# Three engines' instructions issued in the order in which the program writes them: agent attention with a cosine feed-forward on Trainium2

## The chip, the cores and the metric

The kernel runs on one core of a Trainium2 chip. The time is device microseconds of one execution. Before the change it was 1285.07 us (median of 3 runs, 1277.71 to 1285.25).

The core's engines have names in the profile: PE is TensorE (matmuls), PEld its weight loads, DVE is VectorE, ACT is ScalarE, POOL is GpSimd, SP is SyncE, which here issues the DMAs. Each engine takes its own instructions one after the other; an instruction whose input is not ready holds up all that stand behind it on that engine. Engines wait for each other through semaphores.

## What is computed

Cut to what matters, with B = 4 batches, N = 12480 tokens, 128 channels, 49 agents and 2048 hidden units:

```python
def sm(a, b):                       # a softmax of scaled scores
    s = scale * (a @ b.transpose(0, 2, 1))
    s = s - s.max(-1, keepdims=True)
    e = np.exp(s)
    return e / (e.sum(-1, keepdims=True) + 1e-09)

agent_v = sm(agents, k) @ v         # (B, 49, 128)
x = (sm(q, agents) @ agent_v).reshape(B * N, 128)
h = x @ w_in                        # (49920, 2048)
out = (h * np.cos(h)) @ w_out
```

## The kernel before

**Tiles and steps.** Tokens are taken in groups of 960 (`GRP`; 13 groups a batch, 52 in all), each in two chunks of 480 columns. The product of `agent_v` and `w_in` is formed once a batch (`a`), so that a chunk of `h` is one matmul from the 49 softmax weights (`pT`) to 128 hidden units. A step handles 256 hidden units of one chunk: 8 steps a chunk, 16 a group, 208 a batch, 832 in all, and 4 more (`LAG`) to run out. Step n does this (lines 549 to 586):

- TensorE: two matmuls into a `ph` tile (line 558). There are three `ph` tiles in PSUM, so step n needs the one that step n-3 has left.
- ScalarE: the sine with a shift of pi/2, `cos` (line 561), from `ph`.
- VectorE: `r` = (cos - 1) * h (line 563), from `cos` and `ph`. It is the last reader of `ph`.
- `plan.run(n)`: what the plan put at this step (below).
- TensorE: two matmuls of `r` of step n-4 with `w_out` into `po` (line 579). `po` gathers 8 steps; the first of them has none and the second has four, the last adds two correction matmuls (lines 576, 577), then ScalarE copies `po` to `osb` (line 581) and SP stores it.

**The plan.** Everything else of later groups and of the next batch is cut into pieces and put at steps by a schedule written out by hand (lines 465 to 546; `plan`, `extra`, `spread_out`, `burst`). Here a "piece of scores" or "of values" means:

- keys (`ab[b].scores`, line 167): 8 score matmuls a group (16 PE instructions, line 102), half of them in one step and half in the next; ScalarE copies them to `s` (line 181), VectorE keeps a running maximum (line 192);
- queries (`query`, line 351): the same matmuls, then VectorE's maximum and subtraction (lines 360, 367);
- values (`ab[b].values`, line 234): 16 PE instructions (line 244), then VectorE adds the result to `av` (line 247 or 249);
- turned weights (`query_turned`, line 386): four transposes, a ScalarE copy, GpSimd's copies into `pT`, seven steps before the group begins.

All of these results go through the `one` tiles, of which PSUM has two (line 320). `po` holds one of them for most of a chunk, so the pieces share the other, one after the other.

**Bursts.** The exponentials need another ScalarE table than the sine, so they are bundled: at steps 108, 132 and 156 of each of the first three batches (`BURSTS`) stand one exponential of a third of the keys (`pinned_exp`) and one of four or five groups of queries (`query_exp`), with a table load before and after. VectorE's sums over the queries' exponentials (`query_sums`, lines 375 to 377) are planned one step later. Behind the second and the third burst stand four whole pieces of values at four steps on end (line 522), behind the third five more in halves. Two smaller bursts, of queries alone, stand at steps 19 and 732.

**Who sets the order.** The order of the source is not the order on an engine. A scheduler (Tile's) takes the traced instructions and issues each when its modelled inputs and tile buffers are ready, with earlier ones preferred; the semaphores follow from the order that it settles on. `tc.keep_in_program_order(ins)` puts an instruction behind the one that was traced before it on the same engine: an edge for the order of issue, no wait for its end. Before the change it is used for the exponentials (lines 371, 399, 404), and for the loads up to step 7 (line 80).

Of the kernel before, what the change touches and what calls it, by code (L numbers as in the profile page):

```python
# [18 lines left out]
P = 128  # L19
# [21 lines left out]
def agent_attention_cos_ffn(ctx, tc, qT, kT, v, agT, w_in, w_out, outT):  # L41
# [32 lines left out]

    pinned = [True]
# [18 lines left out]
    def scores(sb, src, b, ps):  # L94

        xt = sb.tile([P, GRP], F32, name="xt", bufs=3)
        load(xt, src)
        ps = ps[:TT, :GT * NA].rearrange("p (t a) -> p t a", a=NA)
        for t in range(GT):
            if t == HT:  # L100
                yield
            nc.tensor.matmul(ps[:, t, :], xt[:, t * TT:(t + 1) * TT], ag[:, b, :], start=True, stop=True)  # L102
        return ps

    def scores_twice(xt, src, b, ps):

        load(xt, src)
        ps = ps[:TT, :, :HT * 2 * NA].rearrange("p h (t x a) -> p h t x a", x=2, a=NA)
        for t in range(GT):
            nc.tensor.matmul(ps[:, t // HT, t % HT], xt[:, t * TT:(t + 1) * TT], twice(ag[:, b, :]),  # L110
                             start=True, stop=True)
        return ps[:, :, :, 0, :]

    class Weights:
# [6 lines left out]
        def single(self, src, out):  # L121
# [5 lines left out]
            nc.vector.tensor_scalar(ex, hi, 20, 0x7FF, op0=ALU.logical_shift_right, op1=ALU.bitwise_and)  # L127
            nc.vector.tensor_scalar(man, hi, 0xFFFFF, 0x100000, op0=ALU.bitwise_and, op1=ALU.bitwise_or)
            nc.vector.tensor_scalar(ex, ex, 1151.0, 896.0, op0=ALU.min, op1=ALU.max)
            f = man.bitcast(F32)  # L130
            nc.vector.scalar_tensor_tensor(f, lo, 2.0 ** -32, man, op0=ALU.mult, op1=ALU.add)
            nc.vector.tensor_scalar(ex, ex, 896.0, 2.0 ** 23, op0=ALU.subtract, op1=ALU.mult)
            nc.vector.scalar_tensor_tensor(f, f, 2.0 ** -20, ex.bitcast(F32), op0=ALU.mult, op1=ALU.mult)
            nc.vector.scalar_tensor_tensor(out.bitcast(U32), hi, 0x80000000, man, op0=ALU.bitwise_and, op1=ALU.bitwise_or)
# [5 lines left out]
        def w_out(self, c):  # L140
# [3 lines left out]
            nc.scalar.copy(w1[:, fs], w)  # L144
            return w

        def product(self, c, w, po, wio):

            pt = self.psum()
            for t in range(4):  # L150
                f = slice((4 * c + t) * P, (4 * c + t + 1) * P)
                nc.tensor.transpose(pt[:, t * P:(t + 1) * P], win[:, f], ident)
            wt = self.sb.tile([P, 4, P], F32, name="wt", bufs=2)
            nc.scalar.copy(wt.rearrange("p f d -> p (f d)"), pt)
            for t in range(4):
                nc.tensor.matmul(po, wt[:, t], w[:, t], start=(c == t == 0), stop=(4 * c + t == NF - 1))
            if 4 * c + 4 == NF:
                nc.vector.tensor_copy(wio, po)

    class Agents:  # L160
# [6 lines left out]
        def scores(self, g):  # L167
# [11 lines left out]
            if self.wide is None:  # L179
                ps = yield from scores(sb, src, self.b, self.psum())  # L180
                nc.scalar.copy(s, ps)
            else:
# [5 lines left out]
                nc.scalar.copy(s.rearrange("p (h t) a -> p h t a", h=2), ps)  # L188
            if g == 0:
                nc.vector.tensor_copy(self.run, s)  # L190
            else:
                nc.vector.tensor_max(self.run, self.run, s)  # L192
# [7 lines left out]
        def top(self):  # L200
            self.m = self.sb.tile([TT, NA], F32, name="m", bufs=1)
            nc.vector.tensor_reduce(self.m, self.run.rearrange("p t a -> p a t"), axis=AX.X, op=ALU.max)

        def across(self):
            pt = self.psum()
            nc.tensor.transpose(pt[:NA, :TT], self.m, ident[:TT, :TT])
            mx = self.sb.tile([NA, 1], F32, name="mx", bufs=1)
            nc.vector.reduce_max(mx, pt[:NA, :TT], axis=AX.X)
            self.mxw = self.sb.tile([NA, TT], F32, name="mxw", bufs=1)
            nc.vector.tensor_copy(self.mxw, mx.to_broadcast([NA, TT]))  # L210

        def spread(self):
            pb = self.psum()
            nc.tensor.matmul(pb[:TT, :NA], self.mxw, ident[:NA, :NA], start=True, stop=True)
            self.mxb = self.sb.tile([TT, NA], F32, name="mxb", bufs=1)
            nc.vector.tensor_copy(self.mxb, pb[:TT, :NA])  # L216
# [5 lines left out]
        def exp(self, g, n):  # L222
            e = self.part(g, n)
            return nc.scalar.activation(e, e, AF.Exp, scale=SC)  # L224

        def add(self, g):

            on = nc.vector if self.wide else nc.gpsimd
# [5 lines left out]
        def values(self, g):  # L234
# [6 lines left out]
            for t in range(GT):  # L241
                if t == HT:
                    yield
                nc.tensor.matmul(po, vt[:, t, :], twice(e[:, t, :]), start=(t == 0 and (g == 0 or not lone)),  # L244
                                 stop=(t == GT - 1 and (g == NG - 1 or not lone)))
            if g == (NG - 1 if lone else 0):
                nc.vector.tensor_copy(self.sums, po)
            elif not lone:
                nc.vector.tensor_add(self.sums, self.sums, po)  # L249

        def total(self):
# [3 lines left out]
            nc.vector.tensor_reduce(self.es2[:, :NA], self.es.rearrange("p t a -> p a t"), axis=AX.X, op=ALU.add)  # L255
            nc.vector.tensor_copy(self.es2[:, HI:], self.es2[:, :NA])

        def inverse(self):

            pa = self.psum()  # L260
            nc.tensor.matmul(pa[:KR, :1], self.es2, ones[:TT], start=True, stop=True)
            z = self.sb.tile([KR, 1], F32, name="z", bufs=1)
            nc.vector.tensor_scalar_add(z, pa[:KR, :1], EPS)
            self.rz = self.sb.tile([KR, 1], F32, name="rz", bufs=1)
            nc.vector.reciprocal(self.rz, z)
# [3 lines left out]
    class Fast(Agents):  # L269

        def project(self, c, a):
# [3 lines left out]
            nc.tensor.matmul(pw[:KR], self.av, win[:, cs], start=True, stop=True)  # L275
            if c == 0:
                self.big = self.sb.tile([KR, DFF // 512], F32, name="big", bufs=1)
            nc.scalar.activation(a[:, cs], pw[:KR], AF.Copy, scale=self.rz)
            x = a[:, cs].bitcast(F32)
            nc.vector.tensor_reduce(self.big[:, c:c + 1], x, axis=AX.X, op=ALU.max, apply_absolute_value=True)  # L280

            on = nc.vector if self.wide else nc.gpsimd
            on.tensor_scalar(a[:, cs], x, FAST_MAX, -FAST_MAX, op0=ALU.min, op1=ALU.max)

        def project_out(self, wio, b1, b2):

            pw = self.psum()
            nc.tensor.matmul(pw[:KR, :P], self.av, wio, start=True, stop=True)
            nc.scalar.activation(b1, pw[:KR, :P], AF.Copy, scale=self.rz)
            nc.vector.scalar_tensor_tensor(b2, pw[:KR, :P], self.rz, b1.bitcast(F32), op0=ALU.mult, op1=ALU.subtract)  # L290

        def judge(self):

            t = self.sb.tile([KR, 1], F32, name="t", bufs=1)
            nc.vector.reduce_max(t, self.big, axis=AX.X)
            nc.vector.tensor_scalar(fits[:, self.b:self.b + 1], t, FAST_MAX, None, op0=ALU.is_le)
# [20 lines left out]
    with ExitStack() as pools:  # L317
# [33 lines left out]
        def query(n, piece, wide=False):  # L351
# [8 lines left out]
            nc.vector.reduce_max(mx, ps, axis=AX.X)  # L360
# [6 lines left out]
            nc.vector.tensor_sub(e_of[n].rearrange("p (h t) a -> p h t a", h=2), ps,  # L367
# [5 lines left out]
        def query_sums(piece):  # L373
            rz = rz_of[piece]
            nc.vector.reduce_sum(rz, e_of[piece], axis=AX.X)
            nc.vector.tensor_scalar_add(rz, rz, EPS)
            nc.vector.reciprocal(rz, rz)
# [8 lines left out]
        def query_turned(n):  # L386

            pt = small()
            for t in range(HT):
                nc.tensor.transpose(pt[:KR, t * TT:(t + 1) * TT], p_in[n % 2][:, t, :KR], ident[:TT, :TT])  # L390
            p = sb.tile([KR, CH], F32, name="p")
            nc.scalar.copy(p, pt[:KR, :CH])  # L392
# [8 lines left out]
        def sine_table():  # L401

            t = sb.tile([1, 1], F32, name="sine", bufs=1)
            tc.keep_in_program_order(nc.scalar.activation(t, half_pi[:1], AF.Sin))
# [23 lines left out]
        for j, (g, n) in enumerate(lots):  # L428
            for k in range(g, g + n):
                pre(NG + 2 + k, ab[0].shift, k, 1, nc.vector)  # L430
# [119 lines left out]
        for n in range(NSTEP + LAG):  # L550
            pinned[0] = n < NP
            if n < NSTEP:
# [3 lines left out]
                for j in range(2):  # L556
                    f = slice((2 * i + j) * P, (2 * i + j + 1) * P)
                    nc.tensor.matmul(ph[:, j, :CH], ai[:, f], pTs[q % 3][:, c], start=True, stop=True)  # L558
                h = ph[:, :, :CH]
                cos = sb.tile([P, 2, CH], F32, name="c", bufs=3)  # L560
                nc.scalar.activation(cos, h, AF.Sin, bias=half_pi, scale=1.0)  # L561
                r = rs[n] = sb.tile([P, 2, CH], F32R, name="r", bufs=6)
                nc.vector.scalar_tensor_tensor(r, cos, 1.0, h, op0=ALU.subtract, op1=ALU.mult)  # L563
# [10 lines left out]
            if i == NP - 1:  # L574
                k = q // NG % 2
                nc.tensor.matmul(po, b1[k], pTs[q % 3][:, c], start=False, stop=False)  # L576
                nc.tensor.matmul(po, b2[k], pTs[q % 3][:, c], start=False, stop=False)  # L577
            for f in range(0 if i == 1 else 2 * i, 2 * i + 2):
                nc.tensor.matmul(po, w1[:, f, :], rs[m - i + f // 2][:, f % 2, :], start=(f == 0), stop=(f == NF - 1))  # L579
            if i == NP - 1:  # L580
                nc.scalar.copy(osb[:, c * CH:(c + 1) * CH], po)  # L581
# [6 lines left out]

        bx = sb.tile([KR, 1], F32, name="bx", bufs=1)
        nc.vector.tensor_reduce(bx, fits, axis=AX.X, op=ALU.min)  # L590
        pt = small()
        nc.tensor.transpose(pt[:1, :KR], bx, ident[:KR, :KR])
# [134 lines left out]
```

## Time and profile before

| | |
|---|---|
| median of the runs | 1285.07 us |
| the profiled execution, its own time | 1283.99 us |
| its span, first to last instruction | 1282.0 us |
| before the first matmul of step 0 | 78.3 us |
| granted TensorE clock, mean | 0.966 of full speed |
| PE busy | 1193.2 us (93%) |
| DVE busy | 1096.7 us (86%) |
| ACT busy | 1030.2 us (80%) |
| POOL busy | 316.7 us (25%) |

How to read the lines that are quoted below. A page line of a group is: line of the kernel, engine, operation, tile written and tiles read, shapes, count, then busy time, mean nanoseconds of one, idle time just before them and what ended it. A line of the chain of waits is: who waited for whom, total us, times, the longest. A line of the timeline is: start, duration, engine, line, operation, count when several are merged, and in brackets the idle time before and what ended it. A line of windows is: stretch, its length, then busy time of PE, PEld, DVE, ACT and POOL with counts, the granted clock, the DMA share, GB/s. A matmul of float32 scores shows as two instructions.

### The profile page before, as it was taken

Reading aid. Unit: us, or ns where it says so; the run is one execution under the profiler, and the core shown is the slowest. Engines: PE = TensorE matmul, PEld = TensorE weight load, DVE = VectorE, ACT = ScalarE, POOL = GpSimd, SP = SyncE. Lnnn points to the kernel's source line nnn. Section 1 sums busy time; section 2 is a strip of 40 time slices with the busy share of each in tenths; the row PEclk is TensorE's granted clock in tenths of the full one; section 3 lists DMA queues with packets and bytes.
Section 4 is the critical chain, followed back from the end, with each engine's and each line's share of the span. In section 5 each row is a group of like instructions: output and inputs, shape, how many; then the busy total and the mean of one; then the engine's idle time right before and its main releaser. Section 6 shows DMA issues by size and latency. Waiting matters only on the chain.

```text
span 1282.0 us, 17196 instructions
## 1 busy us (share of the span) xinstructions
PE 1193.2 (93%) x6349; PEld 976.8 (76%) x6349; DVE 1096.7 (86%) x1217; ACT 1030.2 (80%) x1130; POOL 316.7 (25%) x341
## 2 busy tenths in 40 slices
PE   8898999989999999988999999998999999998997
PEld 8787878778887777777888777777778777676664
DVE  6877887788788988879888988887888999998997
ACT  2447887878788877876988888876897999999997
POOL 1202121332222212142422213116241321212220
PEclk9988998989899999998999999997999999998999
DMA  8962323124431223322242222232322010000000
GB/s 306 244 172 76 92 94 93 62 65 126 119 92 62 77 77 94 93 77 77 78 117 74 72 87 80 71 118 62 107 64 63 31 48 31 16 31 16 31 31 34
DMA packets 31016, 107.72 MB, mean 84 GB/s; under 512 B 3436, under 2 KB 3820, under 8 KB 30924
## 3 DMA queue, kind: packets, MB, share of 16 engines
q1 hardware_dynamic: 30924, 106.54, 27.0%
q8 instruction: 52, 0.85, 0.3%
q14 instruction: 40, 0.33, 0.1%
HBM read 80.97 MB, written 25.56 MB: 83 GB/s over the span
## 4 chain that ended last, share of the span: by engine, by line
PE 64%; ACT 14%; DVE 13%; issue 7%; DMA 1%; ACTq 0%; SPq 0%; DVEq 0%
PE ph L558 22%; PE one L579 18%; PE one L102 12%; DVE r L563 10%; ACT c L561 10%; PE one L244 4%; ACT osb L581 2%; PE ph L244 2%; PE one L576 2%; PE one L577 2%; PE ph L110 1%; PE one L390 1%; DVE mx L360 1%; DMA vt<-v 1%; ACT p L392 1%
## 5 line engine op out<-in xcount | busy, mean ns | idle before, releaser
L563 DVE SCALAR_TENSOR_TENSOR r<-c,ph 128x960 fp32r<-128x960 f32 x832 | 929.4, 1149 | 110.1 <-ACT c L561 107.0
L561 ACT ACTIVATE c<-ph,half_pi 128x960 f32<-128x960 f32 x832 | 864.9, 1067 | 172.2 <-PE ph L558 162.0
L558 PE MATMUL ph<-pT,a 113*128 113x480 f32 x1664 | 550.8, 412 | 31.9 <-DVE r L563 28.6
L579 PE MATMUL one<-r,w 128*128 128x480 f32 x1664 | 515.0, 395 | 13.1 <-ACT osb L581 12.0
L558 PEld LDWEIGHTS ph<-pT,a 113*128 113x128 f32 x1664 | 287.3, 194 | 129.8 <-DVE r L563 54.2
L579 PEld LDWEIGHTS one<-r,w 128*128 128x128 f32 x1664 | 317.9, 194 | 71.7 <-ACT osb L581 22.6
L102 PEld LDWEIGHTS one<-ag,xt 128*120 128x120 f32 x1408 | 178.2, 192 | 40.3 <-ACT osb L581 15.1
L102 PE MATMUL one<-ag,xt 128*120 128x49 f32 x1408 | 178.0, 271 | 13.8 <-ACT osb L581 7.6
L381 POOL TENSOR_TENSOR p<-e,rz 120x392 f32<-120x392 f32 x52 | 44.8, 867 | 532.4 <-PE one L390 426.4
L396 POOL TENSOR_TENSOR pT<-p,pT 49x480 fp32r<-49x480 f32 x104 | 127.1, 1222 | 7.9
L395 POOL CAST pT<-p 49x480 fp32r<-49x480 f32 x104 | 63.5, 611 | 167.9 <-ACT p L392 164.4
L244 PEld LDWEIGHTS one<-s,vt 120*128 120x128 f32 x624 | 79.7, 191 | 13.9 <-DVE av L249 6.9
L244 PE MATMUL one<-s,vt 120*128 120x98 f32 x624 | 81.1, 272 | 6.6 <-DVE av L249 4.5
L581 ACT COPY osb<-one 128x480 f32<-128x480 f32 x104 | 57.5, 553 | 4.5 <-PE one L579 4.4
L232 POOL TENSOR_TENSOR es<-es,s 120x392 f32<-120x392 f32 x36 | 36.7, 1019 | 71.5 <-ACT s L224 69.1
L220 POOL TENSOR_TENSOR s<-s,mxb 120x1568 f32<-120x1568 f32 (+1 forms) x9 | 31.6, 3537 | 63.6 <-DVE mxb L216 63.6
L390 PEld LDWEIGHTS one<-ident,p 120*113 120x113 f32 x208 | 31.3, 178 | 17.3 <-ACT osb L581 9.4
L360 DVE TENSOR_REDUCE mx<-one 120x8 f32<-120x392 f32 x49 | 27.5, 562 | 17.6 <-PE one L102 17.2
L390 PE MATMUL one<-ident,p 120*113 120x120 f32 x208 | 36.6, 275 | 6.0 <-ACT osb L581 4.1
L576 PE MATMUL one<-pT,b 113*128 113x480 f32 x104 | 41.3, 397 | 0.0
L577 PE MATMUL one<-pT,b 113*128 113x480 f32 x104 | 40.8, 392 | 0.0
L192 DVE TENSOR_TENSOR run<-run,s 120x392 f32<-120x392 f32 x48 | 27.7, 577 | 5.5 <-ACT s L188 3.1
(91 smaller groups left out, 513.3 us busy)
## 6 DMA issues: line engine op xcount, KB each, us to landing
xt<-qT SPq DMA_DIRECT2D x52, 480.0 KB, 3.5
vt<-v SPq DMA_DIRECT2D x52, 480.0 KB, 4.3
outT<-osb SPq DMA_DIRECT2D x51, 480.0 KB, 2.6
xt<-kT SPq DMA_DIRECT2D x46, 480.0 KB, 3.5
c<-kT SPq DMA_DIRECT2D x6, 480.0 KB, 5.2
raw<-w_in SPq DMA_DIRECT2D x4, 512.0 KB, 5.1
raw<-w_out SPq DMA_DIRECT2D x4, 512.0 KB, 9.1
outT<-osb SPq DMA_DIRECT2D x2, 240.0 KB, 2.7
```

The costliest lines, as they stand in the source:

```text
L102: nc.tensor.matmul(ps[:, t, :], xt[:, t * TT:(t + 1) * TT], ag[:, b, :], start=True, stop=True)
L244: nc.tensor.matmul(po, vt[:, t, :], twice(e[:, t, :]), start=(t == 0 and (g == 0 or not lone)), stop=(t == GT - 1 and (g == NG - 1 or not ...
L390: nc.tensor.transpose(pt[:KR, t * TT:(t + 1) * TT], p_in[n % 2][:, t, :KR], ident[:TT, :TT])
L395: nc.gpsimd.tensor_copy(pT[own, c], p[own])
L396: nc.gpsimd.tensor_sub(pT[other, c], p[own], pT[own, c].bitcast(F32))
L558: nc.tensor.matmul(ph[:, j, :CH], ai[:, f], pTs[q % 3][:, c], start=True, stop=True)
L561: nc.scalar.activation(cos, h, AF.Sin, bias=half_pi, scale=1.0)
L563: nc.vector.scalar_tensor_tensor(r, cos, 1.0, h, op0=ALU.subtract, op1=ALU.mult)
L576: nc.tensor.matmul(po, b1[k], pTs[q % 3][:, c], start=False, stop=False)
L577: nc.tensor.matmul(po, b2[k], pTs[q % 3][:, c], start=False, stop=False)
L579: nc.tensor.matmul(po, w1[:, f, :], rs[m - i + f // 2][:, f % 2, :], start=(f == 0), stop=(f == NF - 1))
L581: nc.scalar.copy(osb[:, c * CH:(c + 1) * CH], po)
```

## The change

From step 0 of the loop on, every instruction that the kernel gives to TensorE, VectorE or ScalarE is put behind the one that was traced before it on its engine. A thin wrapper does it; all calls on the three engines in the functions concerned go through it. What is computed, the tiles, the plan and its steps are the same. GpSimd's instructions and the DMAs (from step 8 on) stay with the scheduler, and so does all that comes ahead of step 0 and behind the loop.

```diff
+    class InOrder:
+        def __init__(self, engine):
+            self.engine = engine
+
+        def __getattr__(self, name):
+            f = getattr(self.engine, name)
+
+            def g(*args, **kwargs):
+                ins = f(*args, **kwargs)
+                if in_order[0]:
+                    tc.keep_in_program_order(ins)
+                return ins
+
+            return g
+
+    in_order = [False]
+    tensor = InOrder(nc.tensor)
+    vector, scalar = InOrder(nc.vector), InOrder(nc.scalar)
...
-                nc.tensor.matmul(po, vt[:, t, :], twice(e[:, t, :]), start=(t == 0 and (g == 0 or not lone)),
+                tensor.matmul(po, vt[:, t, :], twice(e[:, t, :]), start=(t == 0 and (g == 0 or not lone)),
...
             rz = rz_of[piece]
-            nc.vector.reduce_sum(rz, e_of[piece], axis=AX.X)
-            nc.vector.tensor_scalar_add(rz, rz, EPS)
-            nc.vector.reciprocal(rz, rz)
+            vector.reduce_sum(rz, e_of[piece], axis=AX.X)
+            vector.tensor_scalar_add(rz, rz, EPS)
+            vector.reciprocal(rz, rz)
...
         for n in range(NSTEP + LAG):
             pinned[0] = n < NP
+            in_order[0] = True
             if n < NSTEP:
...
-                    nc.tensor.matmul(ph[:, j, :CH], ai[:, f], pTs[q % 3][:, c], start=True, stop=True)
+                    tensor.matmul(ph[:, j, :CH], ai[:, f], pTs[q % 3][:, c], start=True, stop=True)
...
-                nc.scalar.activation(cos, h, AF.Sin, bias=half_pi, scale=1.0)
+                scalar.activation(cos, h, AF.Sin, bias=half_pi, scale=1.0)
...
-                nc.vector.scalar_tensor_tensor(r, cos, 1.0, h, op0=ALU.subtract, op1=ALU.mult)
+                vector.scalar_tensor_tensor(r, cos, 1.0, h, op0=ALU.subtract, op1=ALU.mult)
...
         assert not plan.at
 
+        in_order[0] = False
```

More of the change, by code (lines that the diff above doesn't have):

```diff
@@ L101, in scores @@
                 yield
-            nc.tensor.matmul(ps[:, t, :], xt[:, t * TT:(t + 1) * TT], ag[:, b, :], start=True, stop=True)
+            tensor.matmul(ps[:, t, :], xt[:, t * TT:(t + 1) * TT], ag[:, b, :], start=True, stop=True)
         return ps
@@ L109, in scores_twice @@
         for t in range(GT):
-            nc.tensor.matmul(ps[:, t // HT, t % HT], xt[:, t * TT:(t + 1) * TT], twice(ag[:, b, :]),
+            tensor.matmul(ps[:, t // HT, t % HT], xt[:, t * TT:(t + 1) * TT], twice(ag[:, b, :]),
                              start=True, stop=True)
@@ L187, in scores @@
                 ps = scores_twice(xt, src, self.b, self.wide())
-                nc.scalar.copy(s.rearrange("p (h t) a -> p h t a", h=2), ps)
+                scalar.copy(s.rearrange("p (h t) a -> p h t a", h=2), ps)
             if g == 0:
-                nc.vector.tensor_copy(self.run, s)
+                vector.tensor_copy(self.run, s)
             else:
-                nc.vector.tensor_max(self.run, self.run, s)
+                vector.tensor_max(self.run, self.run, s)
         def copies(self, x):
@@ L403, in sine_table @@
             t = sb.tile([1, 1], F32, name="sine", bufs=1)
-            tc.keep_in_program_order(nc.scalar.activation(t, half_pi[:1], AF.Sin))
+            tc.keep_in_program_order(scalar.activation(t, half_pi[:1], AF.Sin))
         ab = [Fast(sb, small, b, None if b else pair) for b in range(NB)]
@@ L575, in agent_attention_cos_ffn @@
                 k = q // NG % 2
-                nc.tensor.matmul(po, b1[k], pTs[q % 3][:, c], start=False, stop=False)
-                nc.tensor.matmul(po, b2[k], pTs[q % 3][:, c], start=False, stop=False)
+                tensor.matmul(po, b1[k], pTs[q % 3][:, c], start=False, stop=False)
+                tensor.matmul(po, b2[k], pTs[q % 3][:, c], start=False, stop=False)
             for f in range(0 if i == 1 else 2 * i, 2 * i + 2):
-                nc.tensor.matmul(po, w1[:, f, :], rs[m - i + f // 2][:, f % 2, :], start=(f == 0), stop=(f == NF - 1))
+                tensor.matmul(po, w1[:, f, :], rs[m - i + f // 2][:, f % 2, :], start=(f == 0), stop=(f == NF - 1))
             if i == NP - 1:
-                nc.scalar.copy(osb[:, c * CH:(c + 1) * CH], po)
+                scalar.copy(osb[:, c * CH:(c + 1) * CH], po)
                 at = q * GRP
```

92 lines of the change are left out of this document (46 added, 46 removed).

## The prediction

> **What bounds the kernel now.** I read the page's busy times first, then the table of waits, then windows and timelines of three kinds of stretches.
>
> ```profile
> PE 1193.2 (93%) x6349; PEld 976.8 (76%) x6349; DVE 1096.7 (86%) x1217; ACT 1030.2 (80%) x1130; POOL 316.7 (25%) x341
> ```
>
> ```profile
> ACT c L561 <- PE ph L558: 162.0, 267, 4.2
> DVE r L563 <- ACT c L561: 107.0, 236, 1.8
> PE ph L558 <- DVE r L563: 28.6, 59, 4.5
> ```
>
> Three engines are nearly full and wait for each other in a ring: ACT for PE's `ph`, DVE for ACT's `cos`, PE for DVE's `r`. No single engine is the bound; the ring is. Its size comes from a timeline.
>
> ```profile
> 608.54 0.68 PE L558 MATMUL ph<-pT,a 113*128 113x480 f32 x2
> 609.26 1.06 ACT L561 ACTIVATE c<-ph,half_pi 128x960 f32<-128x960 f32 x1 [1.39 <-PE ph L558]
> 610.36 1.16 DVE L563 SCALAR_TENSOR_TENSOR r<-c,ph 128x960 fp32r<-128x960 f32 x1 [1.30 <-ACT c L561]
> ...
> 1208.32 6.57 DVE L563 SCALAR_TENSOR_TENSOR r<-c,ph 128x960 fp32r<-128x960 f32 x6 [0.18 <-ACT c L561]
> ...
> 1212.01 0.59 PE L558 MATMUL ph<-pT,a 113*128 113x480 f32 x2
> 1212.44 0.59 PE L579 MATMUL one<-r,w 128*128 128x480 f32 x2
> ```
>
> From the start of `ph` to the start of its `r` is 610.36 - 608.54 = 1.82 us. With r's own 1.16 and some 0.1 of handing over (an estimate), `ph` of step n, which needs r of step n-3, gives r of step n some 3.1 us after r of n-3 began. Six r in 6.57 us are 1.06 to 1.1 apart, three of them 3.2 to 3.3. So PE may be late with a `ph` by 0.1 to 0.2 us; more shows in the time. A pair of these matmuls takes 0.43 to 0.44 us of PE (1212.01 to 1212.44).
>
> ```profile
> 454.50:548.80 94.30, 89.53 (x506) 74.41 (x506) 80.04 (x84) 75.79 (x86) 17.66 (x19) 1.00 0.31 95
> 1202.30:1265.80 63.50, 60.50 (x251) 42.88 (x251) 61.10 (x57) 60.80 (x67) 11.59 (x13) 1.00 0.08 32
> ```
>
> The second stretch holds steps 768 to 823 without pieces: 63.5 / 56 = 1.134 us a step. The first holds steps 240 to 303 with 14 pieces of scores: 94.3 - 64 x 1.134 = 21.7 us, so a piece costs 1.55 us now.
>
> The third kind is a burst, here the second of a batch (step 340), from the r of step 340 at 610.36:
>
> ```profile
> 610.35 1.28 ACT L224 ACT_TABLE_LOAD   x1
> 611.64 1.51 ACT L224 ACTIVATE s<-s 120x1568 f32<-120x1568 f32 x1
> 612.36 1.92 PE L244 MATMUL one<-s,vt 120*128 120x98 f32 x16
> 613.06 1.50 ACT L371 ACTIVATE e<-e 120x1568 f32<-120x1568 f32 x1
> 614.58 1.28 ACT L561 ACT_TABLE_LOAD   x1
> 614.59 1.79 DVE L375 TENSOR_REDUCE rz<-e 120x32 f32<-120x1568 f32 x1
> 614.63 2.03 PE L244 MATMUL one<-s,vt 120*128 120x98 f32 x16
> 615.87 2.97 ACT L561 ACTIVATE c<-ph,half_pi 128x960 f32<-128x960 f32 x3
> 616.69 0.26 DVE L249 TENSOR_TENSOR av<-av,one 128x98 f32<-128x98 f32 x1 [0.32 <-PE one L244]
> 616.87 0.17 DVE L376 TENSOR_SCALAR rz<-rz 120x32 f32<-120x32 f32 x1
> 617.01 2.03 PE L244 MATMUL one<-s,vt 120*128 120x98 f32 x16 [0.35 <-DVE av L249]
> 617.08 0.35 DVE L377 RECIPROCAL rz<-rz 120x32 f32<-120x32 f32 x1
> 617.35 4.43 DVE L563 SCALAR_TENSOR_TENSOR r<-c,ph 128x960 fp32r<-128x960 f32 x4
> ...
> 621.86 1.15 DVE L563 SCALAR_TENSOR_TENSOR r<-c,ph 128x960 fp32r<-128x960 f32 x1
> ```
>
> ACT makes no cosine for 1.28 + 1.51 + 1.50 + 1.28 = 5.57 us. What matters is what the others do meanwhile. PE runs the values of steps 342, 343 and 344 (the three rows of line 244), which the program writes behind `ph` of those steps. DVE does the sums (lines 375 to 377), which the program writes behind the r of step 341, at 617.35. The scheduler has moved work into the shadow of the burst: from r of 340 to r of 345 pass only 11.5 us.
>
> **The change part by part.** It adds no instruction and no semaphore of its own; it takes the scheduler's freedom on three engines. The four parts:
>
> *Second bursts (steps 132, 340, 548).* In program order DVE has r of 341 ahead of the sums and of the `av` addition, and PE has values 342 ahead of the `po` of step 338 and `ph` of 343. Values 342 need the `one` tile that values 341 used (the other holds `po`), so the `av` addition of 341; that stands behind the sums, those behind r of 341, that behind the cosine after the burst. Behind it on PE waits `ph` of 343, and ACT and DVE for that. In the trace's own times: cosine 341 at 615.87, r 341 at 617.0, sums from 618.1 for 1.79 + 0.17 + 0.35 = 2.3 to 620.4, `av` to 620.6. Values 342 take 1.85 (612.36: 16 in 1.92 with the last one's tail) to 622.5, `po` 0.44, `ph` 343 at 622.95, its r at +1.82 = 624.8. Values 343 run 623.4 to 625.2, `ph` 344 starts 625.65, r 344 at 627.5; values 344 wait for the addition behind r 343 (624.8 + 1.06 + 0.26 = 626.1), end 627.9, `ph` 345 starts 628.35, r 345 at 630.2. It is at 621.86 now: +8.3 us.
>
> *Third bursts (156, 364, 572).* The same with four pieces of values at 365 to 368.
>
> ```profile
> 649.08 2.20 DVE L375 TENSOR_REDUCE rz<-e 120x40 f32<-120x1960 f32 x1 [0.91 <-ACT e L371]
> 650.36 2.97 ACT L561 ACTIVATE c<-ph,half_pi 128x960 f32<-128x960 f32 x3
> ...
> 656.46 2.20 DVE L563 SCALAR_TENSOR_TENSOR r<-c,ph 128x960 fp32r<-128x960 f32 x2
> ```
>
> Cosine 365 at 650.36 gives r at 651.5, the sums run 652.5 to 655.2, `av` to 655.5, and from there to the r of the fourth step after it, 9.6 us as above (620.6 to 630.2): r of 369 at 665.1 instead of 656.46, +8.6 us. Both kinds in three batches: 3 x 16.9 = +51 us. Bounds: +26, if only the sums and one piece of values leave the shadow (2.3 to 2.7 and 1.85, some 4.4 a burst); +56, if each of some eight hand-overs behind a burst takes 0.1 more than I allow.
>
> *Other bursts.* Behind the three first ones stand queries, not values: the sums (2.3) come after r instead of in the shadow, and two pieces that PE now runs early stay at their steps. But the order of now loses there too, with PE waiting for a load (below: 1.31, issue). I take +2 each, +6, between -3 and +5 each. At steps 19 and 732 the sums leave the shadow, 2.3 to 2.9: +6, between 0 and +8.
>
> *All other pieces (103: 39 keys, 49 queries, 15 halved values).* A step with half a piece takes PE 0.44 + 0.86 + 0.44 = 1.74 us, where r's pace is 1.06. Set `ph` of n at 0, just as r of n-3 ends. `ph` of n+1 starts at 1.74, its r at 3.56 instead of 3.09; `ph` of n+2 at 3.48, its r at 5.3 instead of 4.15: late by 1.15. With a query's maximum and subtraction in between, 1.5. A piece that begins three steps after a query waits about 1.0 more for the `one` tile; that is about every eighth. Mean 1.45, against 1.55 now: 103 x -0.1 = -10. Bounds: 0.9 a piece (PE is ahead by more than I allow) is -67, 1.75 is +20. Steps without pieces keep their pace, set by r and the ring in either order: 0. The cover there is DVE's own 1.06; without it a step would have PE's 0.88.
>
> *The clock.* A long wait of PE costs twice.
>
> ```profile
> 573.93 2.93 PE L102 MATMUL one<-ag,xt 128*120 128x49 f32 x16 [1.31 <-issue]
> ...
> 1162.74 2.14 PE L558 MATMUL ph<-pT,a 113*128 113x480 f32 x4 [4.45 <-DVE r L563]
> ```
>
> After 4.45 us of waiting four matmuls take 2.14 us, where two pairs at full clock take 0.44 + 0.6; sixteen score matmuls take 2.93, not 1.85. In the second and third bursts PE now has values to run and the clock stays whole, as the granted clock, 1.00, of the stretch shows:
>
> ```profile
> 610.36:621.86 11.50, 11.15 (x74) 9.88 (x73) 8.44 (x12) 10.60 (x10) 4.09 (x4) 1.00 0.60 163
> ```
>
> In program order PE stands from about 613 (values 341, `po`, `ph` 342 done) to 620.6. So values 342 and the two pairs behind them come at half clock: 1.1 + 0.9 = +2.0 us, six times, +12; between 0 and +20.
>
> On this the Trainium skill, "TensorE: Matmul & The Clock Gate", section "Why this matters for your kernels", says to leave no gaps of over some 3 us between matmuls, since an idle window brings the half clock back. The trace agrees at 1162.74. The page's Part 1 on the clock gate gives the way back as one busy window of about 3.4 us; by that a stretch would lose half of 3.4, an estimate from the page of +1.7 instead of my +2.0, and the sum would be 1347. The same skill, "PSUM — Partial Sum Buffer", section "Engine vs sequencer instructions", says that matmuls start and complete in program order and that the other engines' queues are strict first in, first out; it speaks against the change, as nothing in the chip makes up for an order that has a waiting instruction ahead.
>
> Sum: 51 + 6 + 6 - 10 + 12 = +65 us on the profiled execution's 1284.0 (span 1282.0 and 2.0 around it): 1349 us, 5% slower. The median of the runs is 1.1 above that execution, which changes nothing at this size.
>
> **The rivals.**
>
> *Faster, by an even order.* The plan puts a piece in halves so that no `ph` is over 0.9 us late. The scheduler runs 16 at once:
>
> ```profile
> 550.99 1.88 PE L102 MATMUL one<-ag,xt 128*120 128x49 f32 x16 [0.30 <-ACT osb L581]
> 553.41 3.05 ACT L561 ACTIVATE c<-ph,half_pi 128x960 f32<-128x960 f32 x3 [1.50 <-PE ph L558]
> ```
>
> ACT then waits 1.50, and 162.0 us in all. If halves fit into the ring's slack, a piece costs VectorE's own work, 0.8 us: 103 x -0.75 = -77, and PE, then ahead, has less to catch up behind bursts: half of 51. 1284 + 26 + 12 - 77 = 1245. It decides the sign from about 1.5 us of slack in the ring. Against it: 3.1 against 3.2 to 3.3 us leaves 0.2.
>
> *No change.* The pieces gain what the bursts lose (0.9 a piece), or the edges bind where the scheduler had that order anyway: 1285. Against it: the values and sums named above stand in another order now.
>
> *Worse.* The half clock lasts through the values (16 in 2.93: four pieces +4 a burst, not 2), first bursts cost +5, pieces 1.75: 1284 + 56 + 15 + 8 + 20 + 24 = 1407.
>
> **How the numbers follow.** The forecast, 1310 to 1390 with the inner bounds of its terms: 0.72. Worse, 1390 and up: 0.11. No change: 0.06. Faster: 0.11. The range 1300 to 1390 leaves out about 0.2. Slower by over 1% (about what a measurement of this kernel tells from no change): 0.72 + 0.11 = 0.83; within 1%: 0.06; faster: 0.11.
>
> **What would show it.** In the changed profile, from r of step 340 to r of step 345: about 20 us instead of 11.5, with the sums behind the first r after the burst, and only one piece of values ahead of that r. A line in the waits in which PE at line 244 waits for `av` with several us at a time, and more of ACT's wait for `ph`. A granted clock below 1 in the stretch behind step 340, where it is 1.00 now. Steps 768 to 823 at 1.13 us as before. I am wrong if r of 340 to r of 345 stays under 14 us, or if steps 240 to 303 take under 85 or over 100 us.

## The result, and the profile after

| | before | after |
|---|---|---|
| median of the runs | 1285.16 us (4 runs) | 1366.42 us (4 runs, 1359.72 to 1369.91) |
| ratio | | 1.0637 [1.0575, 1.0699] |
| profiled execution, its span | 1282.0 us | 1362.2 us |
| granted TensorE clock, mean | 0.966 | 0.936 |
| time at half clock, 2 x (1 - clock) x span | 87 us | 174 us |

Slower, by 80.2 us of span. The prediction was 1349 us, +65, within 1300 to 1390. Ratios here and below are those on record, with their 95% interval; they are taken from undisturbed runs alone and can differ a little from the ratio of two medians.

One thing first on how to read what follows: every instruction that goes through the wrapper has the wrapper's line, L85, in the profile. The tiles tell them apart: `ph<-pT,a` is a step's first matmul pair, `one<-r,w` the pair into `po`, `one<-s,vt` the values, `one<-ag,xt` the scores, `rz` the sums, `av` the addition of the values.

The page's busy line, then the table of waits of the kernel after:

```profile
PE 1211.8 (89%) x6349; PEld 997.8 (73%) x6349; DVE 1095.0 (80%) x1217; ACT 1024.2 (75%) x1130; POOL 314.3 (23%) x341
```

```profile
ACT c L85 <- PE ph L85: 242.7, 243, 8.6
DVE r L85 <- ACT c L85: 204.5, 191, 6.1
...
PE one L85 <- DVE av L85: 48.7, 6, 8.7
...
PE one L85 <- DVE m L85: 11.2, 4, 3.3
...
PEld one L85 <- DVE es L85: 10.1, 3, 3.4
```

The engines did the same work in a longer span. The line that stands out is `PE one <- DVE av`: 48.7 us in six waits, 8.1 each, one for each second and third burst (before, 4.5 us in six waits). ACT's wait for `ph` grew from 162.0 to 242.7 and DVE's for the cosine from 107.0 to 204.5: the ring hands the wait on.

Where the time went is read best from one whole batch, between the same steps of both kernels. Windows of the kernel before (r of step 304 to 316, 316 to 336, 386 to 392, and the whole batch 208 to 416; the others stand in the prediction), then of the kernel after (240 to 304, 304 to 316, 316 to 336, 340 to 345, 364 to 369, 386 to 392, 208 to 416, and the quiet 768 to 824):

```profile
548.79:567.95 19.16, 17.01 (x85) 13.30 (x84) 16.37 (x22) 13.41 (x16) 5.86 (x2) 0.91 0.16 53
567.95:603.83 35.88, 31.86 (x156) 26.17 (x156) 28.53 (x33) 26.96 (x27) 17.81 (x17) 0.86 0.23 69
...
679.94:687.98 8.04, 8.04 (x39) 6.62 (x39) 7.39 (x11) 7.19 (x9) 0.96 (x3) 1.00 0.37 122
...
413.48:720.88 307.40, 290.23 (x1576) 240.26 (x1576) 263.87 (x286) 255.33 (x278) 84.28 (x86) 0.98 0.28 84
```

```profile
482.71:572.31 89.60, 86.78 (x507) 74.71 (x505) 80.16 (x85) 74.14 (x86) 16.97 (x19) 1.00 0.32 98
572.31:593.94 21.63, 17.83 (x80) 14.52 (x80) 15.76 (x19) 13.11 (x16) 7.46 (x3) 0.84 0.15 52
593.94:635.25 41.31, 35.04 (x170) 29.02 (x170) 29.31 (x34) 28.09 (x28) 16.19 (x16) 0.83 0.23 69
...
639.69:662.38 22.69, 15.17 (x87) 13.82 (x86) 8.70 (x12) 10.69 (x10) 4.59 (x5) 0.77 0.32 94
...
683.83:707.21 23.38, 14.69 (x86) 13.52 (x86) 9.07 (x12) 11.35 (x10) 5.54 (x6) 0.78 0.27 73
...
731.94:744.43 12.49, 9.53 (x38) 7.25 (x38) 8.74 (x12) 7.33 (x9) 0.20 (x1) 0.86 0.26 79
...
442.01:776.03 334.02, 298.62 (x1578) 248.92 (x1577) 263.43 (x285) 253.34 (x278) 83.44 (x86) 0.93 0.25 77
...
1284.49:1346.20 61.71, 60.33 (x252) 43.11 (x250) 60.51 (x57) 61.23 (x67) 11.67 (x13) 1.00 0.08 33
```

| steps of the batch | before | after | difference |
|---|---|---|---|
| 240 to 304, keys | 94.25 | 89.60 | -4.65 |
| 304 to 316, the maximum's round trip | 19.16 | 21.63 | +2.5 |
| 316 to 336, first burst and what follows | 35.88 | 41.31 | +5.4 |
| 340 to 345, second burst | 11.50 | 22.69 | +11.2 |
| 364 to 369, third burst | 12.26 | 23.38 | +11.1 |
| 386 to 392, the total's round trip | 8.04 | 12.49 | +4.45 |
| the other five stretches | 126.3 | 122.9 | -3.4 |
| 208 to 416 | 307.40 | 334.02 | +26.6 |

The three batches with bursts lost 26.0, 26.6 and 28.0 us, the time ahead of the first r grew by 2.5, and the last batch gained 3.0: together +80.1, with the span at +80.2. (The batches differ in detail: the second burst of the third one takes 22.68 instead of 11.95, its third burst 23.38 instead of 12.24; steps 732 to 737 take 13.7 instead of 10.1.)

The second burst in the timeline of the kernel after, from just before the r of step 340 (639.69). It answers to the burst shown in the prediction:

```profile
639.12 1.92 PE L85 MATMUL one<-s,vt 120*128 120x98 f32 x16
639.67 1.28 ACT L85 ACT_TABLE_LOAD   x1
...
645.19 2.01 ACT L85 ACTIVATE c<-ph,half_pi 128x960 f32<-128x960 f32 x2
646.28 1.16 DVE L85 SCALAR_TENSOR_TENSOR r<-c,ph 128x960 fp32r<-128x960 f32 x1 [5.44 <-ACT c L85]
647.36 1.78 DVE L85 TENSOR_REDUCE rz<-e 120x32 f32<-120x1568 f32 x1
...
649.65 0.20 DVE L85 COPY av<-one 128x98 f32<-128x98 f32 x1
649.77 1.14 DVE L85 SCALAR_TENSOR_TENSOR r<-c,ph 128x960 fp32r<-128x960 f32 x1
649.91 3.73 PE L85 MATMUL one<-s,vt 120*128 120x98 f32 x16 [7.52 <-DVE av L85]
655.09 2.59 PE L85 MATMUL one<-s,vt 120*128 120x98 f32 x16
655.33 1.06 ACT L85 ACTIVATE c<-ph,half_pi 128x960 f32<-128x960 f32 x1 [8.13 <-PE ph L85]
...
658.42 1.92 PE L85 MATMUL one<-s,vt 120*128 120x98 f32 x16
...
662.38 1.15 DVE L85 SCALAR_TENSOR_TENSOR r<-c,ph 128x960 fp32r<-128x960 f32 x1 [1.35 <-ACT c L85]
```

Only one piece of values (639.12) runs while ScalarE makes no cosine. The sums (647.36) and the copy to `av` (649.65) stand behind the first r after the burst. PE waits 7.52 us for that copy, since the next values need its `one` tile; `ph` of step 343 stands behind those values, and so ACT waits 8.13 for it. The values then take 3.73 and 2.59 us, where the last piece takes 1.92.

### The profile page after: what moved, and what is told of

The parts are those of the page before. It is cut to its first block, busy times and chain, and to the rows that moved or that the text cites. A ratio compares the mean times of both kernels' runs of the same rounds, so it can differ in the third digit from the quotient of the medians.

```text
span 1362.2 us, 17172 instructions
## 1 busy us (share of the span) xinstructions
PE 1211.8 (89%) x6349; PEld 997.8 (73%) x6349; DVE 1095.0 (80%) x1217; ACT 1024.2 (75%) x1130; POOL 314.3 (23%) x341
## 4 chain that ended last, share of the span: by engine, by line
PE 58%; DVE 21%; ACT 14%; issue 5%; DMA 1%; ACTq 0%; SPq 0%; DVEq 0%
PE one L85 36%; PE ph L85 22%; DVE r L85 15%; ACT c L85 9%; DVE rz L85 2%; ACT L85 2%; ACT osb L85 1%; DVE e L85 1%; ACT e L391 1%; DVE mx L85 1%; ACT p L85 1%; DMA vt<-v 1%; DVE es L85 0%; DMA raw<-w_out 0%; DVE big L85 0%
## 5 line engine op out<-in xcount | busy, mean ns | idle before, releaser
L85 DVE SCALAR_TENSOR_TENSOR r<-c,ph 128x960 fp32r<-128x960 f32 x832 | 920.1, 1150 | 216.1 <-ACT c L85 204.5
L85 ACT ACTIVATE c<-ph,half_pi 128x960 f32<-128x960 f32 x832 | 859.8, 1068 | 247.5 <-PE ph L85 242.7
L85 PE MATMUL ph<-pT,a 113*128 113x480 f32 x1664 | 541.4, 409 | 50.0 <-DVE r L85 42.4
L85 PE MATMUL one<-r,w 128*128 128x480 f32 x1664 | 520.9, 405 | 1.4 <-ACT osb L85 1.3
L85 PEld LDWEIGHTS ph<-pT,a 113*128 113x128 f32 x1664 | 302.7, 197 | 170.3 <-DVE r L85 87.7
L85 PEld LDWEIGHTS one<-r,w 128*128 128x128 f32 x1664 | 308.4, 196 | 47.0 <-issue 5.0
L85 PEld LDWEIGHTS one<-ag,xt 128*120 128x120 f32 x1408 | 180.1, 190 | 31.2 <-PE ph L85 13.8
L85 PE MATMUL one<-ag,xt 128*120 128x49 f32 x1408 | 173.4, 267 | 11.9 <-PE ph L85 9.7
L85 PE MATMUL one<-s,vt 120*128 120x98 f32 x624 | 91.3, 302 | 48.7 <-DVE av L85 48.7
L85 PEld LDWEIGHTS one<-s,vt 120*128 120x128 f32 x624 | 89.9, 220 | 56.2 <-DVE av L85 53.0
L85 ACT COPY osb<-one 128x480 f32<-128x480 f32 x104 | 58.3, 561 | 26.4 <-PE one L85 26.4
L85 PE MATMUL one<-pT,b 113*128 113x480 f32 x208 | 67.7, 407 | 0.0
L85 PEld LDWEIGHTS one<-pT,b 113*128 113x128 f32 x208 | 37.2, 193 | 5.5 <-issue 1.5
L85 PEld LDWEIGHTS one<-ident,p 120*113 120x113 f32 x208 | 29.1, 180 | 7.0 <-PE ph L85 1.7
L85 PE MATMUL one<-ident,p 120*113 120x120 f32 x208 | 31.0, 271 | 1.1 <-DVE e L85 0.9
L85 PE MATMUL ph<-s,vt 120*128 120x98 f32 x208 | 27.8, 295 | 3.4 <-DMA vt<-v 2.0
```

Source lines behind the costliest of these rows:

```text
L85: ins = f(*args, **kwargs)
```

## The experiments

Three explanations stood against each other. The **burst theory** (the prediction's): five VectorE calls, the three of the sums and the copy or addition to `av`, fall behind the r after a burst and hold back TensorE, whose values leave the burst's shadow. The **queue theory**: it is TensorE's own order, values ahead of `ph` in a queue that goes in order, that loses the time. The **half-clock theory**: the doubled time at half clock is a cause of its own, and not what follows the waits. Unless said otherwise, an edit is made to the kernel after, and a ratio is to the kernel before.

### One engine at a time

```diff
-    vector, scalar = InOrder(nc.vector), InOrder(nc.scalar)
+    vector, scalar = nc.vector, nc.scalar
```

> TensorE alone in program order. Burst theory: VectorE is free to do the sums and the av additions in the shadow of a burst, so values 342 and 343 still run there and only values 344 come after it: r of 340 to r of 345 about 13.5 us (11.5 before, 22.7 with all three); with the round trips of the maximum and of the total still ahead of PE's queue (+2 and +4 a batch) and the even order's gain elsewhere (-20), about 1295 us. Rival, queue theory (PE's in-order queue does the harm by itself): 1350 to 1366 us and some 20 us for that stretch.

Measured: 1295.58 us, 1.0117 [1.004, 1.0193]. The next two keep VectorE's and ScalarE's order alone (`tensor` and the other one plain).

> VectorE alone in program order. Burst theory: the av addition of 341 stands behind the sums and these behind the r after the burst, so values 342 wait for their PSUM tile whatever order PE has; PE can only take other work meanwhile. r of 340 to r of 345 about 17 us, 1310 to 1330 us in all. Queue theory: VectorE's order hardly matters, 1285 to 1295 us.

Measured: 1358.39 us, 1.0608 [1.0538, 1.0678], much more than either theory expected.

> ScalarE alone in program order. Both theories: its order differs from before only by some copies that move by one or two cosines, and the exponentials were pinned already; 1280 to 1290 us, the burst stretch 11 to 12 us.

Measured: 1259.39 us, 0.9822 [0.9753, 0.989], faster than expected.

Windows of r of 340 to r of 345 with TensorE's order alone, and with VectorE's alone:

```profile
616.87:630.17 13.30, 12.06 (x86) 10.82 (x86) 8.44 (x12) 10.59 (x10) 4.56 (x5) 1.00 0.56 166
```

```profile
635.99:655.63 19.64, 13.71 (x69) 11.59 (x69) 8.52 (x13) 11.60 (x10) 4.04 (x4) 0.74 0.23 63
```

TensorE's order by itself costs this burst 1.8 us (13.30 against 11.50), VectorE's 8.1, both 11.2. The queue theory falls: TensorE's fixed queue loses much at these bursts only when VectorE is late with what the head of the queue waits for. And ScalarE's order alone gains 1.8%.

### The five VectorE instructions

First all in order but these five calls:

```diff
-            vector.reduce_sum(rz, e_of[piece], axis=AX.X)
-            vector.tensor_scalar_add(rz, rz, EPS)
-            vector.reciprocal(rz, rz)
+            nc.vector.reduce_sum(rz, e_of[piece], axis=AX.X)
+            nc.vector.tensor_scalar_add(rz, rz, EPS)
+            nc.vector.reciprocal(rz, rz)
...
-                vector.tensor_copy(self.sums, po)
+                nc.vector.tensor_copy(self.sums, po)
...
-                vector.tensor_add(self.sums, self.sums, po)
+                nc.vector.tensor_add(self.sums, self.sums, po)
```

> All three engines in program order but for five VectorE instructions: the three of the sums and the two forms of the av addition, which the scheduler may place. Burst theory, narrowed by the run with VectorE alone (1358 us): these five carry the loss at the bursts. r of 340 to r of 345 from 22.7 to about 13.5 us, 364 to 369 from 23.4 to about 13; with some 2.4 us each at the five bursts of queries, 1366 - 6 x 9.7 - 12 = about 1296 us. Queue theory, in the form that is left (any of VectorE's instructions in its place does harm): 1340 us or more.

Measured: 1286.73 us, 1.0055 [1.003, 1.0079] over 10 runs. Its second burst in the timeline, and the windows of 340 to 345 and 364 to 369:

```profile
615.59 1.92 PE L85 MATMUL one<-s,vt 120*128 120x98 f32 x16
...
617.72 1.78 DVE L395 TENSOR_REDUCE rz<-e 120x32 f32<-120x1568 f32 x1
...
618.25 1.92 PE L85 MATMUL one<-s,vt 120*128 120x98 f32 x16
...
620.65 4.28 DVE L85 SCALAR_TENSOR_TENSOR r<-c,ph 128x960 fp32r<-128x960 f32 x4
```

```profile
613.05:626.37 13.32, 12.08 (x87) 10.84 (x86) 8.44 (x13) 10.59 (x10) 4.57 (x5) 1.00 0.57 162
647.92:660.99 13.07, 12.04 (x86) 11.04 (x86) 9.10 (x12) 11.24 (x10) 5.64 (x6) 1.00 0.48 127
```

The sums are back ahead of the r after the burst, a piece of values takes 1.92 us again, and the granted clock is 1.00 without anything done for it.

The other way round: the kernel before, with these five calls alone kept in program order (they go through `pin`).

```diff
     tensor = nc.tensor
     vector, scalar = nc.vector, nc.scalar
+    pin = InOrder(nc.vector)
...
-            vector.reduce_sum(rz, e_of[piece], axis=AX.X)
+            pin.reduce_sum(rz, e_of[piece], axis=AX.X)
```

> The reverse of the run with five instructions free: the kernel before, and only these five VectorE instructions (the sums, the av additions) kept in program order. Burst theory: enough by itself for most of the loss; 340 to 345 at 19 to 20 us and 364 to 369 at 21 to 22 as with VectorE alone, 1283 + 6 x 8.7 + some 8 at the bursts of queries = about 1343 us. If the loss needs the whole of VectorE's order: under 1310 us.

Measured: 1347.83 us, 1.0509 [1.0471, 1.0548]. The time is right and the place was not: 340 to 345 takes 13.0 us, not 19 to 20. Windows of r of 340 to r of 349, in the kernel before and in this one:

```profile
610.36:626.72 16.36, 15.60 (x94) 13.25 (x92) 12.88 (x17) 15.46 (x16) 6.82 (x8) 1.00 0.44 121
```

```profile
633.07:657.52 24.45, 18.43 (x94) 15.64 (x92) 12.77 (x16) 15.75 (x16) 6.54 (x8) 0.79 0.29 78
```

With TensorE free, the scheduler lets `ph` and r of 341 to 345 pass ahead of the values, and the values come late, three whole pieces behind r of 345, the first of them in part at half clock: 345 to 349 takes 11.4 us instead of 4.85, and the nine steps lose 8.1. Five instructions on VectorE, without an instruction of TensorE pinned, carry most of the loss of the whole change; freeing the same five gives nearly all of it back. The burst theory holds in both directions: these five calls are where the loss starts. The path from there differs: in the kernel after TensorE's queue stands behind the values, and with TensorE free the values themselves come late.

### The values and the sums moved into the shadow by the plan

If program order is what counts, then a program that has the work early should not lose. The four whole pieces of values go to the burst's own step, ahead of the exponentials:

```diff
...
+                    plan(at, lambda g, f=ab[b].values: whole(f(g)), g)
                 for g, n in lots[k:k + 1]:
                     plan(at, pinned_exp, ab[b], g, n)
                 burst(at, ps[k])
...
-                    extra(at + 1, lambda g, f=ab[b].values: whole(f(g)), g, gap=0)
```

> All three in program order, but the four whole pieces of values behind a second or third burst are planned at the burst's own step, ahead of the exponentials (both one-tiles are free there), not at the four steps behind it. Burst theory: three pieces go back into the shadow and PE has no 7 us of waiting, so the clock stays whole there; r of 340 to r of 345 from 22.7 to about 14 us, six such stretches, about 1366 - 50 = 1316 us. If the half clock alone carried the loss, the same. Queue theory: the pieces only move, 1355 to 1366 us.

Measured: 1317.71 us, 1.0301 [1.0232, 1.037]. The timeline has the 64 instructions of the four pieces in one row, with the sums still behind the r, and the stretch 340 to 345 at full clock:

```profile
620.01 7.28 PE L85 MATMUL one<-s,vt 120*128 120x98 f32 x64
...
629.96 1.78 DVE L85 TENSOR_REDUCE rz<-e 120x32 f32<-120x1568 f32 x1
```

```profile
621.40:635.39 13.99, 11.88 (x82) 10.69 (x82) 8.53 (x12) 10.73 (x10) 4.87 (x5) 1.00 0.62 173
```

All four pieces run ahead of and under the burst, and 8.7 of the 11.2 us of this burst are back. TensorE's longest wait there is 2.11 us, and the clock stays whole (in four of the six such bursts it is 0.94 to 0.97). This run doesn't decide on the half-clock theory, since both theories expected the same of it. The trace of the kernel after bounds that theory: TensorE has work at half clock from 649.91 to about 656.5, so the clock can have cost at most 3.3 of the 11.2 us, and the wait of 7.52 us came first. Next the sums too, one step earlier:

```diff
-            plan(t + 1, query_sums, piece)
+            plan(t, query_sums, piece)
```

> All three in program order, with the plan written for it: the four pieces of values at the burst's step as in the run with early values (1317.7), and the sums planned at the burst's step too, ahead of the r behind it. Burst theory: another 2.4 us at each of eleven bursts, 340 to 345 from 14.0 to about 11.6 us, 1317.7 - 27 = about 1291 us. If the sums don't set the time once the values are early: 1315 us.

Measured: 1287.25 us, 1.0026 [0.9999, 1.0053] over 10 runs; 340 to 345 takes 12.60. All three engines are in order, and the loss is gone; what the scheduler did by itself can be written into the plan.

### The two round trips

The prediction had not named the stretches 304 to 316 and 386 to 392. The timeline of the kernel after shows the second:

```profile
736.19 0.81 DVE L85 TENSOR_REDUCE es<-es 120x49 f32<-120x392 f32 x1
...
737.28 0.36 PE L85 MATMUL one<-ones,es 120*113 120x1 f32 x2 [2.96 <-DVE es L85]
```

The matmul on the total `es` is planned a step behind VectorE's reduction, which stands behind an r; TensorE's queue stands 2.96 us for it. In the version of above, `across` and `inverse` go some steps further back from the instruction whose result they need:

```diff
-            t = spread_out(both, t, o + BURSTS[0] - 20)
+            t = spread_out(both, t, o + BURSTS[0] - 24)
...
-            t = extra(t, ab[b].across)
-            t = extra(t + 1, ab[b].spread)
+            t = extra(t + 2, ab[b].across, gap=0)
+            t = extra(t + 2, ab[b].spread, gap=0)
...
-            t = extra(t + 1, ab[b].inverse) + 1
+            t = extra(t + 4, ab[b].inverse) + 1
```

> As the run before, and the two round trips between VectorE and TensorE (transposed maximum, total of the exponentials) planned two and four steps later, so that TensorE's queue doesn't stand in wait for VectorE. By the stretches (386 to 392: 12.5 against 8.0 before the change; 304 to 316: 21.6 against 19.2) some 6 us a batch, 1291 - 19 = about 1272 us. If these waits are hidden: 1291 us.

Measured: 1270.77 us, 0.9882 [0.9825, 0.9939]. Windows of 304 to 316 and 386 to 392:

```profile
680.04:688.47 8.43, 7.19 (x34) 5.36 (x33) 7.68 (x9) 6.62 (x8) 0.00 (x0) 1.00 0.37 117
...
545.37:563.63 18.26, 15.57 (x80) 12.09 (x80) 15.40 (x20) 13.13 (x16) 4.96 (x2) 1.00 0.18 60
```

8.4 instead of 12.5 in the kernel after and in the run before this one: that is the moved matmul on the total, and in three batches it gives 15.2 us. The 18.3 instead of 21.6 are only in part the maximum's: the run before this one, with that wait still at 3.32 us, already had 18.75 there, at a clock of 1.00 instead of 0.84. In three batches the moved maximum takes this stretch from 59.8 to 55.5. With TensorE alone in order, 386 to 392 keeps its 8.05: there the wait needs VectorE's order, and the 4 us a batch that were expected of that run for it did not come. The kernel with all three engines in order is now faster than the kernel before.

### What ScalarE's order gains

With VectorE free, TensorE and ScalarE in order:

```diff
-    vector, scalar = InOrder(nc.vector), InOrder(nc.scalar)
+    vector, scalar = nc.vector, InOrder(nc.scalar)
```

> TensorE and ScalarE in program order, VectorE left to the scheduler. Burst theory: no loss of size at the bursts (13 us at 340 to 345 as with TensorE alone). The gain of ScalarE's order alone (1259 us, not forecast) and the cost of TensorE's alone (1296) should add up if they have different places: about 1272 us; 1259 or less if both come from the same steadier ring.

Measured: 1296.93 us, 1.0115 [1.0084, 1.0147], as with TensorE alone (1.0117). ScalarE's gain does not add to TensorE's order. One place where this kernel loses is shown by windows of steps 448 to 512, here and (the same to 0.01 us) with TensorE alone:

```profile
768.29:866.57 98.28, 94.59 (x505) 80.86 (x503) 79.38 (x84) 74.45 (x86) 16.94 (x19) 0.91 0.28 88
```

The clock of 0.91 stands for 17.1 us at half clock (the last section has the windows), in which PE can lose up to 8.5. With VectorE in order as well, these steps take 89.60, so the half clock is enough to account for nearly all of the difference of 8.7. It starts behind a wait of 1.83 us at step 494. Steps 240 to 304 of the kernel with TensorE alone have the same wait, 1.82 us at step 286, but stay at full clock and take 90.4; here they take 96.7, at 0.93. So a part of what separates these kernels hangs on whether a short wait brings the half clock, told in the last section.

Two parts of ScalarE's order alone, in the kernel before: its 104 copies to `osb`, and its copies to `s` and `p`.

```diff
-                nc.scalar.copy(osb[:, c * CH:(c + 1) * CH], po)
+                tc.keep_in_program_order(nc.scalar.copy(osb[:, c * CH:(c + 1) * CH], po))
```

> The kernel before, and only ScalarE's 104 copies to osb (line 581) kept in program order, so behind the cosine that the scheduler had put them ahead of. On the gain of 1.8% with ScalarE's order alone: if these copies hold up the cosine, and so the ring, 0.2 to 0.25 us each, 1283 - 104 x 0.24 = about 1258 us; if the gain comes from the copies of scores or of turned weights, or from how the schedule falls out, 1275 to 1285 us.

Measured: 1269.28 us, 0.9884 [0.9847, 0.992], between the two forecasts.

```diff
-                nc.scalar.copy(s, ps)
+                pin.copy(s, ps)
...
-            nc.scalar.copy(p, pt[:KR, :CH])
+            pin.copy(p, pt[:KR, :CH])
```

> The kernel before, and only ScalarE's copies of scores to s (line 181) and of turned weights to p (line 392) kept in program order, 91 of them. The copies to osb alone gave 1.2% of the 1.8% that ScalarE's whole order gives. If the rest comes from these copies, and adds up: 1283 - 10 = about 1273 us. If it comes from how the schedules of the three engines fall out together: 1280 to 1290 us, or slower.

Measured: 1264.15 us, 0.9843 [0.9766, 0.9919], faster than both forecasts. The parts gain 1.2% and 1.6%, all of ScalarE 1.8%: they do not add. Either of them takes the keys' stretch, 240 to 304, from 94.25 to 92.0 and 91.6, all of ScalarE to 90.5. So any of these edges leads the scheduler to an order with less waiting (ACT's waits for `ph` in the whole kernel fall from 162.0 to 145 to 147 us in all three); which instruction does it stays open.

### Order only where the plan is even

The runs so far say: program order gains where the plan is spread evenly, and loses at the bursts and round trips. So ScalarE in order throughout, TensorE and VectorE only outside of those (the wrapper takes one flag for ScalarE and one for the other two):

```diff
+            act_order[0] = True
-            in_order[0] = True
+            in_order[0] = 16 <= n and (n % PER < 96 or n % PER >= 200 or n >= 3 * PER) and not 726 <= n < 738
```

> ScalarE in program order from step 0 on; TensorE and VectorE too, but not in the first 16 steps, not from step 96 to 199 of the first three batches (maximum, bursts, values, total) and not at steps 726 to 737. Burst theory: the dense stretches keep 89.6 us for 64 steps, the bursts 11.5 and 12.2 us; adding up the best stretches of the runs so far, ScalarE alone (1259) less 8.6 at steps 32 to 100, 2 at the two other dense stretches and 4 in the last batch: about 1245 us, faster than every kernel so far. If mixed orders upset each other: 1260 to 1280 us.

Measured: 1250.17 us, 0.974 [0.9713, 0.9767] over 6 runs, the fastest of all. Windows of 240 to 304, 340 to 345 and 768 to 824:

```profile
443.00:532.16 89.16, 87.01 (x509) 75.30 (x508) 79.68 (x83) 73.62 (x85) 16.90 (x19) 1.00 0.31 97
...
591.36:602.86 11.50, 11.15 (x74) 9.88 (x73) 8.44 (x12) 10.44 (x9) 4.10 (x4) 1.00 0.67 192
...
1172.84:1234.56 61.72, 60.32 (x252) 43.13 (x250) 60.52 (x58) 61.19 (x67) 11.64 (x13) 1.00 0.08 33
```

The keys' stretch and the quiet stretch have the short times of the kernel after, the burst that of the kernel before. The larger part of the gain is ScalarE's (0.9822 alone); the order of the other two in these stretches adds about 0.8%, and the two intervals just overlap.

## Why the prediction was right, and where it was off

**The bursts: right in mechanism, place and nearly in size.** By the prediction, measured from r of step 340: r of 341 at +6.6, sums from +7.7, `av` done at +10.2, r of 345 at +19.8, or +21.8 with the half clock. The trace has +6.59, +7.67, +10.16 and +22.69. TensorE's wait was to last from 613 to 620.6, 7.6 us; it is 7.52. Second and third bursts were to cost 51 + 12 = 63 us; at 10.7 to 11.2 each, the six of them cost 66. The one miss in size is the half clock, told in the last section.

Behind each of these waits of 7.5 to 8.7 us the clock was half. The Trainium skill, "TensorE: Matmul & The Clock Gate", section "Why this matters for your kernels", warns of such gaps; the trace agrees. At 649.91 PE had 7.52 us to wait and ran nothing of what stood behind. The skill's "PSUM — Partial Sum Buffer", section "Engine vs sequencer instructions", says that matmuls keep program order; by that the order stood as the program had it, and the trace agrees.

**The pieces: right in sign, too small.** Forecast was -0.1 a piece and nothing for a step without one. A quiet step went from 1.134 to 61.71 / 56 = 1.102. With that the keys' stretch has (89.60 - 64 x 1.102) / 14 = 1.36 us a piece instead of 1.55: -0.19, and -0.03 for each step. "Steps without pieces keep their pace" was wrong: 63.5 us became 61.71. That is TensorE's order: alone it brings these steps to 61.7, ScalarE's to 62.6, VectorE's leaves them at 63.5.

**First bursts: too small.** +2 was forecast, between -3 and +5; 316 to 336 lost 5.4, and the other two 5.7. That is just outside the bounds. With only the five VectorE calls pinned, 316 to 323 loses 2.3 and 323 to 336 nothing, so the sums cost what was forecast. The larger part is in 323 to 336: 17.5 us become 21.3 with TensorE's order alone, 22.2 with VectorE's alone and 21.1 with all three. Either order is enough for it, the five calls are not the cause, and which instruction is stays open; the prediction had only a middle value of its bounds for it.

**The step that failed is the list of parts.** It went through bursts and pieces, and left out two places where VectorE gives TensorE a value at once: the maximum and the total. In the loop TensorE waits there three times for the maximum, 9.9 us (the fourth wait of the line, 1.3 us, is ahead of step 0), and (its weight load) three times for the total, 10.1 us. The stretches 304 to 316 and 386 to 392 lost 2.5 and 4.45 us, with their like in the other batches 22.5 us. What the pieces and the steps without one gave back is the remainder, 80.2 - 66.0 (second and third bursts) - 16.8 (first ones) - 22.5 (round trips) - 3.2 (the bursts at steps 19 and 732, -0.4 and +3.6, where +6 was forecast) - 4.2 (up to the first r, 2.5, and steps 0 to 16, 1.7) = -32.5, where -10 was forecast. That the sum, +65 against +80, is nearer than its parts is luck: two errors of opposite sign hid each other.

**The rivals.** "Faster, by an even order" was right on its own stretches (-4.65 us in 64 steps), but not at its price: it asked for -0.75 a piece and for half the bursts' loss. A kernel faster than before comes out once the bursts and round trips are left out of the order of TensorE and VectorE: 0.974, most of it ScalarE's. "No change" is not what happened, but the five instructions freed come to 1.0055, which shows what the loss hung on. "Worse" had the half clock through several pieces of values; it lasts through one and a part of the second.

## What to carry to other kernels

Fixing an order is neither good nor bad: go through the program for every place where one engine's next instruction needs a result that another engine has planned behind work that itself must wait, and price that wait, the small round trips as well as the bursts. A long instruction on one engine casts a shadow; what the scheduler had moved into it must be written there before its freedom is taken away. Where both hold in one kernel, fix the order only in the stretches where the plan is even.

## What the runs showed of the hardware

**Half clock lasts on behind a wait, in whole pieces of 3.41 us.** Windows of the kernel after, around the wait that ends at 649.91:

```profile
642.83:646.24 3.41, 0.00 (x0) 0.00 (x0) 0.00 (x0) 3.38 (x4) 3.08 (x4) 1.00 0.25 84
646.24:656.48 10.24, 6.57 (x27) 6.29 (x28) 4.87 (x8) 2.03 (x3) 0.97 (x1) 0.50 0.17 45
656.48:659.90 3.42, 3.42 (x29) 3.30 (x29) 1.55 (x3) 1.06 (x1) 0.00 (x0) 1.00 0.39 96
```

The clock is half from 646.24, within the wait, to 656.48. PE is busy without a pause from 649.91, and the clock is granted whole again only some 6.5 us later. The prediction's +2.0 us a burst had the values and two pairs in it; 22.69 - 19.8 = 2.9 came out. In each of the traces the clock changes within the loop only on a grid of 3.41 us, so that half clock comes in stretches of 3.4, 6.8, 10.2 us and so on; here they are three pieces of that grid. The Trainium skill, "TensorE: Matmul & The Clock Gate", Part 1, gives at least one busy window of some 3.4 us for the way back, and says that these windows run free of the kernel's start. The trace agrees: of the pieces behind 649.91 the first one that PE fills, 653.07 to 656.48, is the last at half clock.

**A short wait can be enough, and the same wait can do nothing.** The 2.96 us for the total bring 2 x 0.14 x 12.49 = 3.5 us at half clock (clock 0.86 in 386 to 392). With TensorE's order alone, a wait of under 2 us stands at steps 286 and 494; the profile shows nothing that ended it (`issue`). Timeline, then windows, of that kernel:

```profile
522.40 1.01 PE L85 MATMUL one<-ag,xt 128*120 128x49 f32 x8 [1.82 <-issue]
...
832.07 1.76 PE L85 MATMUL one<-ag,xt 128*120 128x49 f32 x8 [1.83 <-issue]
```

```profile
518.10:521.51 3.41, 2.49 (x15) 1.89 (x14) 2.70 (x4) 2.96 (x4) 0.99 (x1) 1.00 0.44 137
521.51:524.93 3.42, 2.53 (x20) 2.43 (x20) 1.85 (x3) 0.71 (x2) 0.00 (x0) 1.00 0.02 7
...
828.71:832.13 3.42, 1.59 (x8) 1.06 (x7) 3.33 (x5) 2.19 (x3) 0.05 (x1) 1.00 0.48 144
832.13:849.20 17.07, 17.07 (x60) 15.20 (x60) 7.63 (x8) 6.85 (x8) 0.00 (x0) 0.50 0.19 59
```

At step 286 the wait falls on two pieces of the grid, PE is busy for 2.49 and 2.53 us in them, and the clock stays whole. At step 494 it falls into one, PE is busy for 1.59 us of it, and half clock follows. In the loops of all the traces half clock followed every piece at full clock in which PE was busy for less than 1.6 us (101 pieces); it also followed 54 in which PE was busy for longer, so this doesn't say all. At step 494 PE is then fully busy for 17 us at half clock. Why it lasts so long here, and 3.4 or 6.5 us elsewhere, the runs don't settle.
